# Linear attention, 32 heads: single warm-up matmuls, the first five heads reordered, and each store cut in three by partitions

## The chip, the core and the metric

The kernel runs on one core of one Trainium2 chip. The time is the device time of one execution in microseconds; the profile shows the core's five engines (PE, the matrix engine; DVE, ACT and POOL, which work on elements; SP, which here only issues DMA transfers) and the 16 DMA engines that move data between HBM and the on-chip memory.

## The reference

```python
# q, k, v: (1, 32, 2048, 128), bf16
phi_q = where(q > 0, q + 1, exp(q)) + 1e-6
phi_k = where(k > 0, k + 1, exp(k)) + 1e-6
kv  = einsum("bhsd,bhse->bhde", phi_k, v)
z   = einsum("bhsd->bhd", phi_k)
num = einsum("bhqd,bhde->bhqe", phi_q, kv)
den = einsum("bhqd,bhd->bhq", phi_q, z)[..., None] + 1e-6
return num / den
```

Each of the 32 heads is on its own: a sum over 2048 rows gives a 128 x 128 matrix kv and a vector z, and every row of q is then multiplied by them and divided.

## The kernel before

A head's q, k and v are 512 KB each and its output is 512 KB. All are laid out on 128 partitions with 16 rows of 128 values (4 KB) on each. The kernel is written out by hand: every piece of work has a name such as `kv3.0` (operation, head, part) and a list of the pieces that it waits for. `ORDER` holds one list per engine, in which that engine does its pieces strictly one after the other. Semaphore waits are made from these lists. So the order within an engine is fixed, and engines wait for one another only where data or a buffer requires it.

The pieces of a head h, with their lines in the profile:

- `ldk`, `ldq`, `ldv` (lines 343 to 348): load of k, q, v, 512 KB each, issued by SP (the v of head 0 by ACT). There are `NI` = 7 input buffers, so a load of head h waits until head h-7 has been used.
- `ek` (360, ACT): exp of k. `em` (363, DVE): min(exp, 1) + 1e-6, in place. `rkp` (370, POOL), and for half of head 0 `rkd` (366, DVE): max(k, 0). phi_k is em + rk, and the two are never added: both go through PE.
- `v1` (374, POOL): v copied beside a column of ones (`v1ones`, 324), so that z is column 128 of the product.
- `kv` (381, PE): 32 matmuls, 16 row blocks times two parts of phi_k, into one PSUM bank. `kvs` (386, DVE): that result to bf16 in the on-chip memory. `kv` of the next head waits for it.
- `T` (393, PE): 16 transposes of q into PSUM. `eq` (397, ACT), `emq` (399, DVE), `rqa` (403, ACT, first half) and `rqb` (406, DVE, second half): the two parts of phi_q from it. `T` of the next head waits for `eq`, `rqa` and `rqb`.
- `n` (417, 422, 424, PE): phi_q times (kv, z), in two groups (`n0.0` of 12 blocks, `n0.1` of 4). `a` (437), `r` (440), `f` (444), all DVE: epsilon, reciprocal, division out of PSUM into one of `NO` = 12 output buffers. `a` of the second group of head h also waits for `kv` of head h+2, because they share a PSUM bank.
- `st` (452, SP): store of the head's output, one transfer of 128 partitions (three for the last head).

Head 0 has k, v and the transposes in two halves. `warm` pieces `w` (329, PE) are matmuls on the identity that nobody uses; they keep PE busy before there is data. `WARM = (2, 8, 4)` is the number in each, and `w2 w1` stand ahead of the first transposes, `w0` behind them.

The program that stands around the orders adds the semaphores: each buffer's transfers count on a semaphore of their own (`o0` to `o11` for the outputs), and a store's completion frees its buffer 12 heads later.

Of the kernel before, what the change touches and what calls it, by code (L numbers as in the profile page):

```python
# [6 lines left out]
P = 128  # L7
EPS = 1e-6
ENGINES = ("PE", "DVE", "ACT", "POOL", "SP")
NH = 32  # L10
BY_ACT = ('ldv0.0',)
NI, NO, NE, NR, NV, NQ, NK = 7, 12, 2, 2, 2, 2, 2
WARM = (2, 8, 4)
HALVES = ((0, 8), (8, 16))
WHOLE = ((0, 16),)

# [41 lines left out]
def groups(h):  # L58
    if h == NH - 1:
        return ((0, 2, 3, 0), (6, 2, 3, 2), (12, 2, 2, 4))  # L60
    return ((0, 4, 3, 0), (12, 2, 2, 4))


def st_parts(h):
    return ((0, 6), (6, 12), (12, 16)) if h == NH - 1 else WHOLE


# [20 lines left out]
def rqb_parts(h):  # L88
    if na(h) == 16:
        return ()  # L90
    if h == NH - 1:
# [3 lines left out]

ORDER = {
    "PE": """
        w2 w1 T0.0 T0.1 w0 T1.0 kv0.0 kv0.1 n0.0 kv1.0 T2.0 n0.1 kv2.0 n1.0 n1.1 T3.0 kv3.0 n2.0 T4.0 n2.1 kv4.0
        n3.0 T5.0 n3.1 kv5.0 n4.0 T6.0 n4.1 kv6.0 n5.0 T7.0 n5.1 kv7.0 n6.0 T8.0 n6.1 kv8.0 n7.0 T9.0 n7.1 kv9.0
        n8.0 T10.0 n8.1 kv10.0 n9.0 T11.0 n9.1 kv11.0 n10.0 T12.0 n10.1 kv12.0 n11.0 T13.0 n11.1 kv13.0 n12.0  # L100
        T14.0 n12.1 kv14.0 n13.0 T15.0 n13.1 kv15.0 n14.0 T16.0 n14.1 kv16.0 n15.0 T17.0 n15.1 kv17.0 n16.0
        T18.0 n16.1 kv18.0 n17.0 T19.0 n17.1 kv19.0 n18.0 T20.0 n18.1 kv20.0 n19.0 T21.0 n19.1 kv21.0 n20.0
        T22.0 n20.1 kv22.0 n21.0 T23.0 n21.1 kv23.0 n22.0 T24.0 n22.1 kv24.0 n23.0 T25.0 n23.1 kv25.0 n24.0
        T26.0 n24.1 kv26.0 n25.0 T27.0 n25.1 kv27.0 n26.0 T28.0 n26.1 kv28.0 n27.0 T29.0 n27.1 kv29.0 n28.0
        T30.0 n28.1 kv30.0 n29.0 T31.0 T31.1 n29.1 kv31.0 n30.0 n30.1 n31.0 n31.1 n31.2
    """,
    "DVE": """
        eps0 ones emq0.0 em0.0 em0.1 rqb0.0 rkd0.0 v1ones0 v1ones1 eps1 emq0.1 em1.0 eps2 kvs0 emq1.0 r0.0
        rqb1.0 em2.0 kvs1 f0.0 em3.0 a0.1 r0.1 kvs2 f0.1 rqb2.0 r1.0 f1.0 emq2.0 em4.0 a1.1 r1.1 rqb3.0 f1.1
        r2.0 kvs3 f2.0 emq3.0 em5.0 a2.1 r2.1 rqb4.0 f2.1 r3.0 kvs4 f3.0 emq4.0 em6.0 a3.1 r3.1 rqb5.0 f3.1 r4.0  # L110
        kvs5 f4.0 emq5.0 em7.0 a4.1 r4.1 rqb6.0 f4.1 r5.0 kvs6 f5.0 emq6.0 em8.0 a5.1 r5.1 rqb7.0 f5.1 r6.0 kvs7
        f6.0 emq7.0 em9.0 a6.1 r6.1 rqb8.0 f6.1 r7.0 kvs8 f7.0 emq8.0 em10.0 a7.1 r7.1 rqb9.0 f7.1 r8.0 kvs9
        f8.0 emq9.0 em11.0 a8.1 r8.1 rqb10.0 f8.1 r9.0 kvs10 f9.0 emq10.0 em12.0 a9.1 r9.1 rqb11.0 f9.1 r10.0
        kvs11 f10.0 emq11.0 em13.0 a10.1 r10.1 rqb12.0 f10.1 r11.0 kvs12 f11.0 emq12.0 em14.0 a11.1 r11.1
        rqb13.0 f11.1 r12.0 kvs13 f12.0 emq13.0 em15.0 a12.1 r12.1 rqb14.0 f12.1 r13.0 kvs14 f13.0 emq14.0
        em16.0 a13.1 r13.1 rqb15.0 f13.1 r14.0 kvs15 f14.0 emq15.0 em17.0 a14.1 r14.1 rqb16.0 f14.1 r15.0 kvs16
        f15.0 emq16.0 em18.0 a15.1 r15.1 rqb17.0 f15.1 r16.0 kvs17 f16.0 emq17.0 em19.0 a16.1 r16.1 rqb18.0
        f16.1 r17.0 kvs18 f17.0 emq18.0 em20.0 a17.1 r17.1 rqb19.0 f17.1 r18.0 kvs19 f18.0 emq19.0 em21.0 a18.1
        r18.1 rqb20.0 f18.1 r19.0 kvs20 f19.0 emq20.0 em22.0 a19.1 r19.1 rqb21.0 f19.1 r20.0 kvs21 f20.0 emq21.0
        em23.0 a20.1 r20.1 rqb22.0 f20.1 r21.0 kvs22 f21.0 emq22.0 em24.0 a21.1 rqb23.0 r21.1 f21.1 r22.0 kvs23  # L120
        f22.0 emq23.0 em25.0 a22.1 r22.1 rqb24.0 f22.1 r23.0 kvs24 f23.0 emq24.0 em26.0 a23.1 r23.1 rqb25.0
        f23.1 r24.0 kvs25 f24.0 emq25.0 em27.0 a24.1 r24.1 rqb26.0 f24.1 r25.0 kvs26 f25.0 emq26.0 em28.0 a25.1
        r25.1 rqb27.0 f25.1 r26.0 kvs27 f26.0 emq27.0 em29.0 a26.1 r26.1 rqb28.0 f26.1 r27.0 kvs28 f27.0 emq28.0
        em30.0 a27.1 r27.1 rqb29.0 f27.1 kvs29 r28.0 emq29.0 f28.0 em31.0 a28.1 kvs30 rqb30.0 r28.1 f28.1 r29.0
        emq30.0 f29.0 emq31.0 emq31.1 a29.1 r29.1 kvs31 f29.1 emq31.2 r30.0 f30.0 a30.1 r30.1 f30.1 r31.0 f31.0
        a31.1 r31.1 r31.2 f31.1 f31.2
    """,
    "ACT": """
        exp ldv0.0 ek0.0 ek0.1 eq0.0 eq0.1 rqa0 ek1.0 eq1.0 ek2.0 rqa1 ek3.0 eq2.0 rqa2 ek4.0 eq3.0 rqa3 ek5.0
        eq4.0 rqa4 ek6.0 eq5.0 rqa5 ek7.0 eq6.0 rqa6 ek8.0 eq7.0 rqa7 ek9.0 eq8.0 rqa8 ek10.0 eq9.0 rqa9 ek11.0  # L130
        eq10.0 rqa10 ek12.0 eq11.0 rqa11 ek13.0 eq12.0 rqa12 ek14.0 eq13.0 rqa13 ek15.0 eq14.0 rqa14 ek16.0
        eq15.0 rqa15 ek17.0 eq16.0 rqa16 ek18.0 eq17.0 rqa17 ek19.0 eq18.0 rqa18 ek20.0 eq19.0 rqa19 ek21.0
# [2 lines left out]
        eq30.0 rqa30 eq31.0 eq31.1 eq31.2 rqa31  # L135
    """,
    "POOL": """
        ident0 ident rkp0.0 rkp1.0 v10.0 v10.1 v11.0 rkp2.0 v12.0 rkp3.0 v13.0 v14.0 rkp4.0 v15.0 rkp5.0 v16.0
        rkp6.0 v17.0 rkp7.0 rkp8.0 v18.0 rkp9.0 v19.0 rkp10.0 v110.0 v111.0 rkp11.0 v112.0 rkp12.0 v113.0
        rkp13.0 v114.0 rkp14.0 v115.0 rkp15.0 v116.0 rkp16.0 rkp17.0 v117.0 rkp18.0 v118.0 v119.0 rkp19.0 v120.0  # L140
        rkp20.0 rkp21.0 v121.0 rkp22.0 v122.0 rkp23.0 v123.0 rkp24.0 v124.0 rkp25.0 v125.0 v126.0 rkp26.0 v127.0
        rkp27.0 v128.0 rkp28.0 v129.0 rkp29.0 v130.0 rkp30.0 rkp31.0 v131.0
    """,
    "SP": """
        ldk0.0 ldq0.0 ldk1.0 ldk2.0 ldq1.0 ldv1.0 ldk3.0 ldv2.0 ldq2.0 ldq3.0 ldk4.0 ldv3.0 ldv4.0 ldv5.0 ldk5.0
        ldv6.0 ldq4.0 ldk6.0 ldq5.0 ldk7.0 ldv7.0 ldk8.0 ldk9.0 ldv8.0 ldq6.0 ldq7.0 ldk10.0 ldv9.0 st0.0 ldq8.0
        ldv10.0 ldv11.0 ldk11.0 ldq9.0 ldq10.0 ldv12.0 ldq11.0 ldk12.0 ldk13.0 ldv13.0 ldq12.0 ldq13.0 ldq14.0
        ldq15.0 ldv14.0 ldv15.0 ldq16.0 ldk14.0 ldk15.0 ldk16.0 ldv16.0 ldv17.0 ldk17.0 st1.0 st2.0 ldq17.0
        ldq18.0 ldk18.0 ldv18.0 ldk19.0 ldv19.0 ldk20.0 ldq19.0 st3.0 ldv20.0 ldv21.0 st4.0 ldq20.0 ldk21.0
        ldq21.0 st5.0 ldk22.0 st6.0 ldq22.0 st7.0 st8.0 ldv22.0 ldk23.0 ldk24.0 ldv23.0 ldk25.0 ldv24.0 ldk26.0  # L150
        ldv25.0 st9.0 ldq23.0 st10.0 st11.0 st12.0 ldq24.0 ldk27.0 ldv26.0 ldk28.0 ldq25.0 ldv27.0 st13.0
        ldk29.0 ldq26.0 ldq27.0 ldk30.0 ldv28.0 st14.0 ldv29.0 st15.0 ldq28.0 ldv30.0 ldq29.0 ldk31.0 st16.0
        ldq30.0 st17.0 st18.0 st19.0 ldv31.0 st20.0 ldq31.0 st21.0 st22.0 st23.0 st24.0 st25.0 st26.0 st27.0
        st28.0 st29.0 st30.0 st31.0 st31.1 st31.2
    """,
}

# [10 lines left out]
class Program:  # L168
# [10 lines left out]
    def add(self, eng, key, fn, deps=(), dma=None, inc=True):  # L179
        assert key not in self.op, key  # L180
        self.op[key] = (eng, fn, tuple(deps), dma, inc)
# [71 lines left out]
def bass_standalone__linear_attn_elu__prompt_kernel(nc: bass.Bass, q: bass.AP, k: bass.AP, v: bass.AP, out: bass.AP):  # L253
# [8 lines left out]
    qf, kf, vf, of = (t.rearrange("b h s d -> (b h) s d") for t in (q, k, v, out))  # L262
    rows = lambda t, h: t[h].rearrange("(p j) d -> p j d", j=NT)

    with ExitStack() as es:
# [17 lines left out]
        o_sb = sb([P, NO, NT, D])  # L283
        ident, ones, epsr = sb([P, P]), sb([P, P]), sb([P, 3])
# [7 lines left out]
        add = pr.add  # L292
# [33 lines left out]
        def warm(key, n):  # L326
            def g(e):
                for w in range(n):
                    ins = e.matmul(o_ps[:, 512:992], lhsT=ident[:], rhs=_ap(ident[:, :], 0, [[0, 4], [1, 120]]),  # L329
                                   start=(w == 0), stop=(w == n - 1))  # L330
                return ins
            add("PE", key, g, ["ident"], inc=False)

        for i, n in enumerate(WARM):
            warm(f"w{i}", n)
# [15 lines left out]
        def head(h):  # L351
# [58 lines left out]
            for i, (t0, nb, m, b0) in enumerate(groups(h)):  # L410
# [31 lines left out]
                def g(e, t0=t0, t1=t1, nb=nb, m=m, b0=b0):  # L442
# [5 lines left out]
                        in1=_ap(rden_sb[:, :, :], first(rden_sb[:, h % 2, t0:t0 + 1]) - first(rden_sb[:, :, :]),  # L448
                                [[m, nb], [1, m], [0, D]]), op=ALU.mult)
                add("DVE", f"f{h}.{i}", g, [f"r{h}.{i}"] + freed(NO, h, ("st", st_parts)))  # L450
            for i, (a, b) in enumerate(st_parts(h)):
                add("SP", f"st{h}.{i}", lambda e, a=a, b=b: e.dma_start(rows(of, h)[:, a:b], o_sb[:, h % NO, a:b]),
                    [f"f{h}.{j}" for j, (t0, nb, m, b0) in enumerate(groups(h)) if t0 < b and a < t0 + nb * m],
                    dma=f"o{h % NO}")

        for h in range(NH):
            head(h)
# [40 lines left out]
```

## Time and profile before

| | |
|---|---|
| median of 3 runs | 169.61 us (169.48 to 169.76) |
| the profiled execution | 170.02 us |
| its span, first to last instruction | 168.6 us |
| mean granted PE clock | 0.983 |
| busy: PE, DVE, ACT, POOL | 155.6, 153.7, 149.6, 93.4 us |
| moved by DMA | 67.51 MB, mean 400 GB/s |
| HBM read, written | 50.33 MB, 16.78 MB |

The span is the time between the first and the last instruction of the profiled execution. Busy time is the union of an engine's instructions. Matmuls are pipelined, so one that is listed with 220 ns starts about 56 ns after the one before it, and PE's pace is read from starts and not from durations. "GB/s" and the DMA share count what all 16 DMA engines move in a stretch; a share slightly over 1 means that packets overlap a little.

### The profile page before, as it was taken

The page shows a single profiled execution, that of the slowest core. Times are in us where ns is not written, and L with a number is a line of the kernel's source. Part 1 is how long each engine was busy: PE and PEld are TensorE (multiplying, and loading weights), DVE is VectorE, ACT ScalarE, POOL GpSimd, SP SyncE. Part 2 cuts the span into 40 slices and gives each one's busy share as a digit, 9 for nine tenths or more (in the row PEclk, how much of TensorE's full clock was granted, in tenths as well). Part 3 has the DMA queues.
Part 4 walks back from the last instruction along what each step waited for, and adds up shares of the span by engine and source line. Part 5 has one row for each costly group of instructions (what it writes and reads, how often), then busy time and mean ns, then how long its engine had stood idle before and what let it go on. Part 6 is the DMA issues. An engine that isn't in the chain of part 4 may idle for free.

```text
span 168.6 us, 6160 instructions
## 1 busy us (share of the span) xinstructions
PE 155.6 (92%) x2702; PEld 151.2 (90%) x2702; DVE 153.7 (91%) x300; ACT 149.6 (89%) x102; POOL 93.4 (55%) x71
## 2 busy tenths in 40 slices
PE   6809999999999999999999999999999999999940
PEld 2309999999999999999999999999999999999940
DVE  0093999999999999999999999999999999999993
ACT  3784799999999999999999999999999999996800
POOL 1380895566666555555566666555555667642000
PEclk9996999999999999999999999999999999999997
DMA  5999999999999999999999999999999999999985
GB/s 206 431 420 424 385 431 393 412 412 406 416 400 412 408 404 408 390 436 402 395 429 419 408 421 425 417 389 430 433 406 404 412 445 390 420 417 414 391 326 225
DMA packets 9819, 67.51 MB, mean 400 GB/s; under 512 B 2080, under 2 KB 2464, under 8 KB 6816
## 3 DMA queue, kind: packets, MB, share of 16 engines
q1 hardware_dynamic: 9648, 66.59, 96.8%
q8 instruction: 21, 0.34, 0.8%
q10 hardware_dynamic: 144, 0.52, 0.8%
q14 instruction: 6, 0.05, 0.1%
HBM read 50.33 MB, written 16.78 MB: 398 GB/s over the span
## 4 chain that ended last, share of the span: by engine, by line
PE 88%; DVE 6%; DMA 3%; ACT 1%; issue 0%; SPq 0%
PE la L381 35%; PE la L422 18%; PE la L393 17%; PE la L424 17%; DMA la<-in_q_dram 3%; DVE la L444 3%; DVE la L399 1%; DVE la L363 1%; ACT la L397 1%; DVE la L440 1%; PE la L417 0%; DVE la L406 0%; SPq L348 0%; DVE la L386 0%; DVE la L437 0%
## 5 line engine op out<-in xcount | busy, mean ns | idle before, releaser
L444 DVE TENSOR_TENSOR la<-la 128x1536 bf16<-128x1536 f32 (+2 forms) x65 | 77.7, 1197 | 0.2
L370 POOL TENSOR_SCALAR la<-la 128x2048 bf16<-128x2048 bf16 (+1 forms) x32 | 59.7, 1866 | 29.3 <-PE la L381 23.8
L424 PE MATMUL la<-la 128*128 128x129 bf16 x512 | 67.0, 220 | 0.0
L422 PE MATMUL la<-la 128*128 128x129 bf16 x512 | 67.0, 219 | 0.0
L397 ACT ACTIVATE la<-la 128x2048 bf16<-128x2048 bf16 (+2 forms) x35 | 60.2, 1730 | 6.0 <-PE la L393 3.3
L360 ACT ACTIVATE la<-la 128x2048 bf16<-128x2048 bf16 (+1 forms) x33 | 61.3, 1860 | 3.8 <-PE la L381 2.0
L381 PE MATMUL la<-la 128*128 128x129 bf16 x1024 | 64.4, 222 | 0.0
L381 PEld LDWEIGHTS la<-la 128*128 128x128 bf16 x1024 | 60.5, 99 | 0.0
L374 POOL COPY la<-la 128x1024 int32<-128x1024 int32 (+1 forms) x33 | 34.4, 1043 | 29.5 <-PE la L381 25.5
L424 PEld LDWEIGHTS la<-la 128*128 128x128 bf16 x512 | 49.6, 97 | 0.0
L422 PEld LDWEIGHTS la<-la 128*128 128x128 bf16 x512 | 47.9, 97 | 0.2 <-DVE la L444 0.2
L393 PE MATMUL la<-la 128*128 128x128 bf16 x512 | 34.5, 222 | 4.6 <-DVE la L406 4.2
L393 PEld LDWEIGHTS la<-la 128*128 128x128 bf16 x512 | 30.4, 99 | 5.8 <-ACT la L360 4.6
L403 ACT ACTIVATE la<-la 128x1024 bf16<-128x1024 bf16 (+1 forms) x32 | 33.5, 1046 | 0.0
L399 DVE TENSOR_SCALAR la<-la 128x2048 bf16<-128x2048 bf16 (+2 forms) x35 | 25.3, 724 | 7.3 <-ACT la L397 7.3
L363 DVE TENSOR_SCALAR la<-la 128x2048 bf16<-128x2048 bf16 (+1 forms) x33 | 23.9, 726 | 0.0
L417 PE MATMUL la<-la 128*128 128x3 bf16 (+1 forms) x128 | 21.6, 169 | 2.1 <-DVE la L444 1.7
L406 DVE TENSOR_SCALAR la<-la 128x1024 bf16<-128x1024 bf16 x31 | 20.5, 662 | 0.0
L417 PEld LDWEIGHTS la<-la 128*128 128x128 bf16 x128 | 12.5, 98 | 2.4 <-DVE la L444 1.8
L440 DVE RECIPROCAL la<-la 128x12 f32<-128x12 f32 (+2 forms) x65 | 13.0, 201 | 1.1
L386 DVE CAST la<-la 128x129 bf16<-128x129 f32 x32 | 7.8, 243 | 2.6 <-PE la L381 2.6
L329 PE MATMUL la<-la 128*128 128x480 bf16 x14 | 5.2, 546 | 1.5 <-POOL la L314 1.5
(16 smaller groups left out, 10.7 us busy)
## 6 DMA issues: line engine op xcount, KB each, us to landing
la<-in_k_dram SPq DMA_DIRECT2D x32, 512.0 KB, 17.5
la<-in_q_dram SPq DMA_DIRECT2D x32, 512.0 KB, 18.2
la<-in_v_dram SPq DMA_DIRECT2D x31, 512.0 KB, 18.5
out_dram<-la SPq DMA_DIRECT2D x31, 512.0 KB, 19.1
la<-in_v_dram ACTq DMA_DIRECT2D x1, 512.0 KB, 4.9
out_dram<-la SPq DMA_DIRECT2D x2, 192.0 KB, 2.6
out_dram<-la SPq DMA_DIRECT2D x1, 128.0 KB, 2.8
```

The lines of the kernel that those rows point to most:

```text
L360: add("ACT", f"ek{h}.{i}", lambda e, a=a, b=b: e.activation(em_sb[:, h % NE, a:b], k_sb[:, h % NI, a:b], ACT.Exp), over("ldk", h, ld_parts ...
L370: add("POOL", f"rkp{h}.{i}", lambda e, a=a, b=b: e.tensor_scalar(rk_sb[:, h % NR, a:b], k_sb[:, h % NI, a:b], BIG, 0.0, op0=ALU.min, op1=A ...
L374: add("POOL", f"v1{h}.{i}", lambda e, a=a, b=b: e.tensor_copy(v1_sb[:, h % NV, a:b, 0:D].bitcast(i32), v_sb[:, h % NI, a:b].bitcast(i32)), ...
L381: ins = e.matmul(kv_ps, lhsT=src[:, j], rhs=v1_sb[:, h % NV, j, 0:NC], start=(j + part == 0), stop=(j == NT - 1 and part == 1))
L393: ins = e.transpose(xT[:, j], q_sb[:, h % NI, j], ident[:])
L397: add("ACT", f"eq{h}.{i}", lambda e, a=a, b=b: e.activation(emq_sb[:, h % NQ, a:b], xT[:, a:b], ACT.Exp), over("T", h, t_parts, a, b) + fr ...
L399: add("DVE", f"emq{h}.{i}", lambda e, a=a, b=b: e.tensor_scalar(emq_sb[:, h % NQ, a:b], emq_sb[:, h % NQ, a:b], 1.0, EPS, op0=ALU.min, op1 ...
L403: add("ACT", f"rqa{h}", lambda e: e.activation(rq_sb[:, h % NQ, 0:n], xT[:, 0:n], ACT.Relu), over("T", h, t_parts, 0, n) + freed(NQ, h, (" ...
L417: e.matmul(_ap(o_ps[:, :], o + D, [[NC, m]]), lhsT=ones[:], rhs=epsr[:, 0:m], start=True, stop=False, skip_group_check=True)
L422: e.matmul(to, lhsT=emq_sb[:, h % NQ, t], rhs=kvs_sb[:, h % NK, 0:NC], start=late and c == 0, stop=False, skip_group_check=True)
L424: ins = e.matmul(to, lhsT=rq_sb[:, h % NQ, t], rhs=kvs_sb[:, h % NK, 0:NC], start=False, stop=True, skip_group_check=True)
L444: return e.tensor_tensor(out=_ap(o_sb[:, :, :, :], first(o_sb[:, h % NO, t0, 0:1]) - first(o_sb[:, :, :, :]), [[m * D, nb], [D, m], [1, D] ...
```

## The change

Three things are changed.

The warm-up becomes 17 pieces: sixteen of a single matmul and one of 12. The piece of 12 and nine single ones stand ahead of the first transposes, two behind each half of these and four between `kv0.1` and `T1.0` (28 matmuls in all instead of 14).

The orders of the first five heads are new on all engines. On PE, `kv0` stands ahead of `T1.0`; on ACT, `ek1.0` ahead of `eq0.0`; on DVE, the memsets, `em0.0`, `rkd0.0` and `em0.1` ahead of `emq0.0`. On POOL, `rkp` and `v1` alternate through nearly all heads.

The stores of heads 0 to 21 become three transfers each, of partitions 0 to 47, 48 to 95 and 96 to 127, whole rows of 4 KB as before. In SP's order they stand between the loads from the 16th SP transfer on. Before, `st0.0` came behind 28 loads and `st1.0` behind 24 more.

```diff
-WARM = (2, 8, 4)
+WARM = (1, 1, 1, 1, 1, 1, 1, 1, 1, 1, 1, 1, 1, 1, 1, 1, 12)
...
+ROWS = ((0, 48), (48, 96), (96, 128))
+
+def st_rows(h, i):
+    return ROWS[i] if len(st_parts(h)) == len(ROWS) and h < NH - 1 else (0, P)
+
 def st_parts(h):
+    if h < 22:
+        return WHOLE * len(ROWS)
     return ((0, 6), (6, 12), (12, 16)) if h == NH - 1 else WHOLE
...
 PE
-        w2 w1 T0.0 T0.1 w0 T1.0 kv0.0 kv0.1 n0.0 kv1.0 T2.0 n0.1 kv2.0 n1.0 n1.1 T3.0 kv3.0 n2.0 T4.0 n2.1 kv4.0
+        w16 w6 w4 w7 w8 w9 w1 w10 w11 w12 T0.0 w0 w13 T0.1 w2 kv0.0 kv0.1 w14 w5 w3 w15 T1.0 kv1.0 n0.0 n0.1
+        T2.0 kv2.0 n1.0 T3.0 n1.1 kv3.0 n2.0 T4.0 n2.1 kv4.0 ...
 DVE
-        eps0 ones emq0.0 em0.0 em0.1 rqb0.0 rkd0.0 v1ones0 v1ones1 eps1 emq0.1 em1.0 eps2 kvs0 emq1.0 r0.0
-        rqb1.0 em2.0 kvs1 f0.0 em3.0 a0.1 r0.1 kvs2 f0.1 rqb2.0 r1.0 f1.0 ...
+        v1ones0 eps0 v1ones1 eps1 ones em0.0 rkd0.0 eps2 em0.1 emq0.0 em1.0 rqb0.0 emq0.1 kvs0 em2.0 kvs1 rqb1.0
+        r0.0 f0.0 emq1.0 em3.0 a0.1 r0.1 rqb2.0 f0.1 r1.0 kvs2 f1.0 ...
 ACT
-        exp ldv0.0 ek0.0 ek0.1 eq0.0 eq0.1 rqa0 ek1.0 eq1.0 ek2.0 rqa1 ek3.0 ...
+        exp ldv0.0 ek0.0 ek0.1 ek1.0 eq0.0 eq0.1 rqa0 ek2.0 eq1.0 rqa1 ek3.0 ...
 SP
-        ldk0.0 ldq0.0 ldk1.0 ldk2.0 ldq1.0 ldv1.0 ldk3.0 ldv2.0 ldq2.0 ldq3.0 ldk4.0 ldv3.0 ldv4.0 ldv5.0 ldk5.0
-        ldv6.0 ldq4.0 ldk6.0 ldq5.0 ldk7.0 ldv7.0 ldk8.0 ldk9.0 ldv8.0 ldq6.0 ldq7.0 ldk10.0 ldv9.0 st0.0 ldq8.0
...
-        ldq30.0 st17.0 st18.0 st19.0 ldv31.0 st20.0 ldq31.0 st21.0 st22.0 st23.0 ...
+        ldk0.0 ldq0.0 ldk1.0 ldk2.0 ldv1.0 ldq1.0 ldv2.0 ldk3.0 ldq2.0 ldv3.0 ldq3.0 ldk4.0 ldv4.0 ldk5.0 ldq4.0
+        st0.0 ldv5.0 ldq5.0 st0.1 ldk6.0 ldq6.0 st0.2 ldv6.0 st1.0 ldk7.0 ldv7.0 st1.1 ldq7.0 ldk8.0 st1.2
...
+        st17.1 st17.2 ldq29.0 st18.0 st18.1 st18.2 ldk31.0 st19.0 ldq30.0 st19.1 st19.2 st20.0 ldq31.0 st20.1
+        st20.2 st21.0 ldv31.0 st21.1 st21.2 st22.0 st23.0 ...
...
-                add("SP", f"st{h}.{i}", lambda e, a=a, b=b: e.dma_start(rows(of, h)[:, a:b], o_sb[:, h % NO, a:b]),
+                add("SP", f"st{h}.{i}", lambda e, a=a, b=b, p=st_rows(h, i): e.dma_start(
+                    rows(of, h)[p[0]:p[1], a:b], o_sb[p[0]:p[1], h % NO, a:b]),
                     [f"f{h}.{j}" for j, (t0, nb, m, b0) in enumerate(groups(h)) if t0 < b and a < t0 + nb * m],
```

## The prediction

> **What bounds the kernel now.** I read the page first (queues, slices), then the windows view by stage, then the chain and the timelines of the start. The page's DMA queues and its slices of DMA share and rate:
>
> ```profile
> q1 hardware_dynamic: 9648, 66.59, 96.8%
> q8 instruction: 21, 0.34, 0.8%
> ...
> DMA  5999999999999999999999999999999999999985
> GB/s 206 431 420 424 385 431 393 412 412 406 416 400 412 408 404 408 390 436 402 395 429 419 408 421 425 417 389 430 433 406 404 412 445 390 420 417 414 391 326 225
> ```
>
> The 16 DMA engines idle only in the first slice and the last two. By stage (stretch, length, busy time of PE, PEld, DVE, ACT, POOL; granted clock, DMA share, GB/s):
>
> ```profile
> 12.00:16.00 4.00, 3.69 (x37) 3.72 (x38) 2.17 (x8) 1.88 (x1) 0.80 (x1) 0.57 0.98 397
> 43.00:57.00 14.00, 14.00 (x258) 14.00 (x256) 13.90 (x29) 13.90 (x10) 8.78 (x7) 1.00 1.01 407
> 73.00:100.00 27.00, 27.00 (x495) 27.00 (x493) 26.80 (x55) 26.82 (x19) 16.61 (x13) 1.00 1.02 416
> 100.00:122.00 22.00, 22.00 (x404) 22.00 (x402) 21.86 (x43) 21.84 (x15) 13.28 (x10) 1.00 1.02 420
> 160.00:166.00 6.00, 2.19 (x38) 1.91 (x36) 5.65 (x11) 0.19 (x1) 0.00 (x0) 1.00 0.80 320
> ```
>
> PE, DVE, ACT and DMA are all full. A stretch of loads alone (43 to 57) moves 407 GB/s, loads mixed with stores 416 to 420. At 414 GB/s the 67.1 MB need 162 us from the first packet at 1.8, so 4 to 5 us of the span is all that DMA has to spare, most of it at the end.
>
> PE's own clock is set at the start. The chain in order of time (start, length, what) has T1.0 at 12.31 and then the kv matmuls of heads 0, 1, 3 and 4:
>
> ```profile
> 12.31 1.66 PE la L393 x16
> 13.97 2.85 PE la L381 x32
> 18.83 1.81 PE la L381 x32
> 26.93 1.81 PE la L381 x32
> 31.55 1.81 PE la L381 x32
> ```
>
> T1.0 and kv0 run at half clock (0.57 above) after 4.2 us of idle PE; from head 3 on a head takes 4.62 us with no gap until 160. DVE's timeline shows what the start waits for: emq0.0, which takes 1.77 us where its twin emq0.1 takes 0.41, because it ends only after POOL's rkp1.0 has (9.84).
>
> ```profile
> 8.35 1.77 DVE L399 TENSOR_SCALAR la<-la 128x1024 bf16<-128x1024 bf16 x1 [7.32 <-ACT la L397]
> 16.84 0.30 DVE L386 CAST la<-la 128x129 bf16<-128x129 f32 x1 [2.62 <-PE la L381]
> ```
>
> Which of the two clocks sets the end? Each transfer's semaphore is raised 16 times, once by each DMA engine, and the trace records each. The slowest engine finishes ldq31.0 (the 117th transfer) at 154.35 and the last store at 168.59: 13 transfers of 11 stores' bytes, 1.29 us per store, no gap. DMA sets the end, and PE's last work arrives just in time for it.
>
> **Warm-up and first heads.** T0.0 now stands behind 12 warm-up matmuls (end near 6.0, as before) and 9 more at 0.20 us (line 329 at full clock): 7.8 instead of 6.63. That is hidden: ACT does ek1.0 first, from k1's landing (7.9) to 9.75, so eq0.0 begins there. If the clock came late, 9 at 0.40 would add 1.8 us, and eq0.0 would move by 0.1. kv0 no longer waits for T1.0: its last input is v10.0, half of a 1.04 us copy behind rkp1.0, so it begins near 10.5 and ends at 12.3, not 16.8. T1.0 waits for rqb0.0 behind em1.0: 13.5. kv1 waits for kvs0, which DVE has behind emq0.1, which waits for POOL's rkp2.0 to end (14.7): kv1 at 15.3. From there, with 1.81 for kv, 0.89 for T and 4.62-1.81-0.89 = 1.92 for n, kv3 begins 9.24 us later, at 24.5 instead of 26.93. PE gains 2.4 us, some 1.8 of it the cold clock ((1.66-0.89) + (2.85-1.81)). The POOL reorder costs nothing (55% busy), nor do the memsets put first on DVE, idle until 5. It is worth 2.4 us only if loads and stores keep up.
>
> The Trainium skill, "TensorE: Matmul & The Clock Gate", part 1, has the clock fall after an idle window of about 3.4 us, so the gaps of about 1 us left here would be harmless; no row here has such a gap that early.
>
> **st0 on SP's queue.** SP issues in order. Before, st0 was the 29th transfer on SP, waiting until 25.24 with some 18 us of loads already queued. Now 16 loads are issued by 10 and SP stops at st0.0, with ldv5.0 and all later loads behind it. st0.0 waits for f0.1, whose a0.1 waits for kv2 (ends 15.3+1.81+1.92+0.89+1.81 = 21.7); a, r, rqb2.0 and f0.1 make it 23.45. The 16th load lands at 23.1 on the median engine. A store of 192 KB into an empty queue first lands 1.8 us after issue (the last head's, 163.93 to 165.76), so at 25.3; without a gap it would have landed at 23.1+0.48. Idle DMA: 1.7, say 1.8 us; 1.1 on an engine that lags (its 16th load lands at 24.4). Bounds: 0.8 if f0.1 comes a microsecond earlier, 2.8 if later. Nothing hides it, as DMA sets the end. From there st1.0 finds 3 us queued: no second gap.
>
> **Splitting and interleaving.** From one transfer's landing on the fastest engine to the next one's, 6th to 119th transfer:
>
> ```
> previous, this    times  us after the previous one
> load, load           75  1.272
> load, store          16  1.249
> store, load          15  1.199
> store, store          7  1.231
> ```
>
> A load behind a store is 0.073 us cheaper, a store behind a load 0.018 dearer than behind a store. In the stages with many stores a load takes 1.25 to 1.26 even behind a load; I take 1.25. From st0's place to the end of st21 the old order has 80 loads and 22 stores, 22.84 to 150.86 = 128.0 us. In the new one 56 loads stand directly behind a store part, 24 behind a load; 57 parts behind a load. So 56 x 1.199 + 24 x 1.25 + 22 x 1.231 + 57 x 0.018 = 67.1 + 30.0 + 27.1 + 1.0 = 125.2: 2.8 us less. 44 more semaphore packets at 9 ns each per engine: +0.4. No row shows a store of 48 or 32 partitions, nor a load behind one. Bounds for such a load: 1.199 if the saving belongs to the change of direction, 1.248 if it goes by bytes (a third of 0.073). I take the first: after three stores in a row (st10 to st12, then ldq24.0) it is 1.21, no better than after one. SP's 44 further issues of 0.35 us fit into its waits.
>
> Sum: -2.8 + 0.4 + 1.8 = -0.6 us. The last load is ldv31.0, behind 21 3/8 stores where ldq31.0 had 21: it lands at 154.35 - 0.6 + 0.5 = 154.2, v131 takes 1.04, so kv31 begins at 155.4, 0.8 earlier than now: PE agrees with DMA. The other 1.6 us that PE could gain go into waiting for loads, at lines 360, 370, 374 or 393.
>
> The Trainium skill, "DMA: Bandwidth & Descriptors", rules for kernel authors, speaks against the split: two transfers to disjoint partitions share the same 16 engines, so use one of 128 partitions. By that rule alone the split brings nothing and the sum is that of the first rival; the rows above favour it only as mixing.
>
> The profiled execution took 170.02 us, 1.4 more than its span of 168.6, and lies 0.41 above the median of 169.61; the change is taken against that median: 169.0.
>
> **Rivals.** *Slower: the cheaper load goes by bytes.* 56 x 0.049 = +2.7, so +2.1: 171.7. It decides once a load behind a part takes over 1.210 us (1.199 + 0.6/56). For it: the trace's 16 KB load packets take 637 ns with no store packet beside them and 614 to 628 with some, so it is company that helps, and a third of a store gives it a third as long. Chance 0.30. *Slower: parts of 48 partitions move more slowly than 159 ns per 4 KB packet*, the figure of every store here. Each 10% costs 22 x 1.27 x 0.1 = 2.8 us; it decides from 2%. Nothing in the profile shows it. 172 and more, chance 0.10. *Much faster: DMA stops being the bound*, with 1.20 for every load (-1.2 more) and half of the gap. Then PE's 2.4 us hold: 167.2. Chance 0.12. *No change:* the terms cancel within 0.34 us, the 0.2% that a measurement of this kernel can tell: 0.14.
>
> **Numbers.** Forecast 169.0, chance 0.34 (168.0 to 169.2). Range 167.2 to 171.8: it leaves out the slow parts and little else. Faster 0.34 + 0.12, same 0.14, slower 0.30 + 0.10.
>
> **What would show it.** Right: clock 1.00 from 12 to 16; kv1 near 15.3, kv3 near 24.5; st0.0 issued near 23.5 and a dip of the DMA share around 23 to 25; 418 GB/s or more from 26 to 150; heads a little over 4.62 us apart with waits for loads. Wrong: 410 GB/s or less in that stretch (first rival), store packets over 159 ns (second), 4.62 us per head to the end (third), or no dip.

## The result, and the profile after

The changed kernel takes 172.55 us (172.52 to 172.92, 4 runs) against 169.67 us (169.48 to 169.76, 4 runs) for the kernel before on the same chip: ratio 1.0169, 95% interval 1.0154 to 1.0184. It is 2.9 us slower; the forecast was 169.0, and the time lies above the range. The profiled execution took 172.52 us, its span is 171.2 us (168.6 before), and the mean granted clock is 0.997 (0.983 before). In the views of the changed kernel the lines are 12 or 13 further down: `ek` is 373, `rkp` 383, `v1` 387, `kv` 394, `T` 406, `eq` 410, `emq` 412.

The start first. The chain in order of time of the changed kernel (start, length, what), from ACT's `ek1.0` to `kv1`:

```profile
8.25 1.45 ACT la L373
9.70 0.37 issue
10.07 1.01 ACT la L410
11.10 0.47 DVE la L412
11.58 1.44 DVE la L376
13.02 0.60 DVE la L419
13.62 1.51 DVE la L412
15.12 0.21 DVE la L399
15.38 1.99 PE la L394 x32
```

It is the chain that the prediction described: `emq0.1` (13.62) takes 1.51 us where `emq0.0` takes 0.47, while POOL is in `rkp2.0` (12.95 to 14.84); `kvs0` (15.12) stands behind it, and `kv1` starts at 15.38.

The changed kernel's DMA queues and slices show what went wrong:

```profile
q1 hardware_dynamic: 10352, 66.60, 95.7%
q8 instruction: 21, 0.34, 0.8%
...
DMA  5999959999999999999999999999999999999976
GB/s 208 424 417 413 410 178 313 368 438 398 441 414 412 412 420 419 416 418 412 419 418 415 428 395 433 404 419 427 411 420 428 409 409 421 421 407 406 400 310 240
```

A slice is 4.28 us. The DMA share has one hole, in the sixth slice (178 GB/s), but the next two slices, with the engines busy again by their share, still move only 313 and 368. The windows view of the changed kernel (stretch, length, busy time of PE, PEld, DVE, ACT, POOL; granted clock, DMA share, GB/s):

```profile
12.00:16.00 4.00, 3.36 (x47) 2.51 (x45) 4.00 (x5) 4.00 (x3) 3.52 (x3) 1.00 0.99 401
20.00:24.00 4.00, 4.00 (x77) 4.00 (x75) 3.97 (x10) 3.78 (x3) 2.25 (x3) 1.00 0.63 254
24.00:28.00 4.00, 4.00 (x77) 4.00 (x75) 3.97 (x7) 3.97 (x4) 2.25 (x2) 1.00 0.91 262
28.00:32.00 4.00, 4.00 (x77) 4.00 (x75) 3.96 (x9) 3.97 (x3) 1.58 (x2) 1.00 0.98 344
32.00:36.00 4.00, 4.00 (x76) 4.00 (x73) 4.00 (x8) 3.92 (x4) 1.97 (x2) 1.00 1.00 414
43.00:57.00 14.00, 12.84 (x227) 12.31 (x225) 13.93 (x24) 12.39 (x9) 9.05 (x7) 1.00 1.01 416
73.00:100.00 27.00, 27.00 (x494) 27.00 (x492) 26.79 (x53) 26.81 (x18) 16.52 (x13) 1.00 1.01 416
100.00:122.00 22.00, 22.00 (x403) 22.00 (x401) 21.86 (x43) 20.78 (x15) 12.99 (x9) 1.00 1.02 418
160.00:166.00 6.00, 4.28 (x74) 3.76 (x72) 5.83 (x15) 2.65 (x3) 0.00 (x0) 1.00 0.85 343
```

From 12 to 16 PE now has the full clock (0.57 before). From 28 to 32 the DMA share is 0.98 at 344 GB/s: busy engines, slow packets. From 43 to 122 the rate is 416 to 418, and in 43 to 57 PE is idle 1.2 of 14 us where it had no idle before.

PE's inputs come late: POOL and ACT, which prepare them, wait longer for loads. The waits view covers the whole span (us in total, times, longest). Of the changed kernel:

```profile
POOL la L383 <- DMA la<-in_k_dram: 22.8, 11, 3.8
POOL la L387 <- DMA la<-in_v_dram: 7.8, 4, 4.1
ACT la L373 <- DMA la<-in_k_dram: 6.7, 5, 2.1
```

and of the kernel before:

```profile
POOL la L370 <- DMA la<-in_k_dram: 5.4, 2, 2.8
POOL la L374 <- DMA la<-in_v_dram: 3.9, 3, 2.5
ACT la L360 <- DMA la<-in_k_dram: 1.9, 1, 1.9
```

PE's 2.2 us lead over the kernel before is there until head 6 (`kv6` at 38.50 against 40.71), is gone at head 9, and is a delay of 1.40 us from head 10 and of 2.45 us at the last (`kv31` at 158.67 against 156.22).

What DMA has moved for loads and stores, from the packet records of both traces:

```
MB moved by            34 us   60 us   100 us   150 us
before                 13.02   23.57    39.96    60.65
after                  11.46   22.28    38.85    59.58
behind, MB              1.56    1.29     1.11     1.07
the same at 414 GB/s   3.8 us  3.1 us   2.7 us   2.6 us
```

All of the loss is there at 34 us; after that the new order gains 1.2 us back. 2.6 us are left, and 2.6 us is what the span has grown by.

### The profile page after: what moved, and what is told of

Same layout as the page of the kernel before. It is cut to its first block, busy times and chain, and to the rows that moved or that the text cites. A ratio compares the mean times of both kernels' runs of the same rounds, so it can differ in the third digit from the quotient of the medians.

```text
span 171.2 us, 6223 instructions
## 1 busy us (share of the span) xinstructions
PE 158.3 (92%) x2716; PEld 151.1 (88%) x2716; DVE 155.7 (91%) x300; ACT 149.7 (87%) x102; POOL 95.1 (56%) x71
## 4 chain that ended last, share of the span: by engine, by line
DVE 65%; PE 24%; DMA 4%; ACT 4%; issue 2%; SPq 0%
DVE la L457 30%; DVE la L376 10%; PE la L394 10%; DVE la L412 10%; DVE la L419 8%; PE la L406 5%; PE la L435 5%; PE la L437 4%; DVE la L453 4%; DMA la<-in_k_dram 4%; DVE la L399 2%; ACT la L410 2%; DVE la L450 1%; ACT la L416 1%; ACT la L373 1%
## 5 line engine op out<-in xcount | busy, mean ns | idle before, releaser
L383 POOL TENSOR_SCALAR la<-la 128x2048 bf16<-128x2048 bf16 (+1 forms) x32 | 60.8, 1901 | 53.2 <-PE la L394 30.4
L394 PEld LDWEIGHTS la<-la 128*128 128x128 bf16 x1024 | 59.2, 98 | 2.2 <-issue 1.3
L437 PEld LDWEIGHTS la<-la 128*128 128x128 bf16 x512 | 49.5, 97 | 0.0
L435 PEld LDWEIGHTS la<-la 128*128 128x128 bf16 x512 | 47.8, 97 | 0.3 <-DVE la L399 0.3
L387 POOL COPY la<-la 128x1024 int32<-128x1024 int32 (+1 forms) x33 | 35.0, 1064 | 9.5 <-DMA la<-in_v_dram 7.8
L406 PE MATMUL la<-la 128*128 128x128 bf16 x512 | 34.0, 219 | 2.9 <-DVE la L419 1.9
L406 PEld LDWEIGHTS la<-la 128*128 128x128 bf16 x512 | 29.8, 98 | 4.5 <-DVE la L419 2.9
L376 DVE TENSOR_SCALAR la<-la 128x2048 bf16<-128x2048 bf16 (+1 forms) x33 | 26.1, 791 | 4.1 <-ACT la L373 4.0
L430 PEld LDWEIGHTS la<-la 128*128 128x128 bf16 x128 | 12.5, 97 | 3.0 <-DVE la L457 2.0
L342 PE MATMUL la<-la 128*128 128x480 bf16 x28 | 8.7, 469 | 1.5 <-POOL la L327 1.5
```

What stands on the lines that cost most here:

```text
L376: add("DVE", f"em{h}.{i}", lambda e, a=a, b=b: e.tensor_scalar(em_sb[:, h % NE, a:b], em_sb[:, h % NE, a:b], 1.0, EPS, op0=ALU.min, op1=AL ...
L383: add("POOL", f"rkp{h}.{i}", lambda e, a=a, b=b: e.tensor_scalar(rk_sb[:, h % NR, a:b], k_sb[:, h % NI, a:b], BIG, 0.0, op0=ALU.min, op1=A ...
L387: add("POOL", f"v1{h}.{i}", lambda e, a=a, b=b: e.tensor_copy(v1_sb[:, h % NV, a:b, 0:D].bitcast(i32), v_sb[:, h % NI, a:b].bitcast(i32)), ...
L394: ins = e.matmul(kv_ps, lhsT=src[:, j], rhs=v1_sb[:, h % NV, j, 0:NC], start=(j + part == 0), stop=(j == NT - 1 and part == 1))
L406: ins = e.transpose(xT[:, j], q_sb[:, h % NI, j], ident[:])
L435: e.matmul(to, lhsT=emq_sb[:, h % NQ, t], rhs=kvs_sb[:, h % NK, 0:NC], start=late and c == 0, stop=False, skip_group_check=True)
```

## The experiments

Three theories: the gap behind `st0.0` and the slow stretch that follows it cost the time (A); the parts of 48 and 32 partitions do (B); the new start does (C). Within A: is it the stop itself, or something that comes with it? Each kernel is compared with the kernel before, run beside it on the same chip (median 169.95 us for runs 1 to 4, 170.05 for 5 to 8, 170.03 for 9 to 11, 169.89 for 12).

**1. The start alone.** The changed kernel with SP's order of before and whole stores.

```diff
 def st_parts(h):
-    if h < 22:
-        return WHOLE * len(ROWS)
...
 SP
-        ldk0.0 ldq0.0 ldk1.0 ldk2.0 ldv1.0 ldq1.0 ... ldk5.0 ldq4.0 st0.0 ldv5.0 ldq5.0 st0.1 ...
+        ldk0.0 ldq0.0 ldk1.0 ldk2.0 ldq1.0 ldv1.0 ... ldk10.0 ldv9.0 st0.0 ldq8.0 ldv10.0 ldv11.0 ...
...
```

> The new warm-up and the new orders of PE, DVE, ACT and POOL, with the old order of SP and whole stores. Theory A (the loss sits in the DMA gap behind st0.0, 22 to 34 us, and in what it costs to start again): st0 has its 23 loads ahead, no gap, kv3 near 24.6 as in the changed kernel, and PE keeps its lead of about 2 us as long as the loads of the old order allow: 167.5 to 169.3 us. Theory B (the split transfers are slow in themselves): the same here, since nothing is split. Theory C (the new start costs more than it saves, for instance by making every later wait fall badly): 170 us or more.

Measured 169.78 us, ratio 0.9993 (0.9983 to 1.0004). `kv3` is 3.2 us earlier than before, `kv10` still 1.85, and from head 24 on the lead melts: `kv31` is 0.28 later. The windows view of this kernel has PE waiting in 122 to 148:

```profile
122.00:148.00 26.00, 24.74 (x444) 24.30 (x442) 24.20 (x47) 23.87 (x17) 14.75 (x11) 1.00 1.01 414
```

The time lies between what A and C forecast. The start costs nothing (not C) and, with DMA's order unchanged, brings nothing: PE runs into DMA. The transposes of heads 24, 25, 26 and 28 each start 0.09 us after their q has landed (`T28` at 141.11, its q at 141.02). In the kernel before, `T28` starts at 141.01 with its q there since 140.75, so the old order of loads has hardly any lead to give.

**2. Whole stores at the new places.** The changed kernel, each store of heads 0 to 21 whole at its first part's place.

```diff
-    if h < 22:
-        return WHOLE * len(ROWS)
...
-        ... st0.0 ldv5.0 ldq5.0 st0.1 ldk6.0 ldq6.0 st0.2 ldv6.0 st1.0 ...
+        ... st0.0 ldv5.0 ldq5.0 ldk6.0 ldq6.0 ldv6.0 st1.0 ...
```

> The changed kernel with each store of heads 0 to 21 whole, in the place of its first part; the loads stay in their order. Theory A: the gap behind st0.0 stays, with about 4 us of DMA work lost in it, and there are fewer changes of direction: 172 to 174 us, DMA at 250 to 350 GB/s from 24 to 32 us. Theory B: the parts were the cost, so 170 us or less, and the rate after the gap comes back at once.

Measured 173.28 us, ratio 1.0198 (1.0166 to 1.0229). The windows view of this kernel shows the same hole and the same slow stretch without any part:

```profile
20.00:24.00 4.00, 4.00 (x77) 4.00 (x75) 3.96 (x10) 3.76 (x3) 2.25 (x3) 1.00 0.62 250
24.00:28.00 4.00, 4.00 (x77) 4.00 (x75) 3.97 (x7) 3.97 (x4) 2.26 (x3) 1.00 0.93 336
28.00:32.00 4.00, 4.00 (x76) 4.00 (x74) 3.96 (x9) 3.97 (x3) 2.12 (x3) 1.00 0.94 336
32.00:36.00 4.00, 4.00 (x75) 4.00 (x74) 4.00 (x8) 3.97 (x4) 1.38 (x1) 1.00 0.97 358
```

The parts are not the cause of the hole or of the slow stretch (not B).

**3. Stores eight loads later.** The changed kernel, parts and all, with `st0.0` behind 24 loads instead of 16; the shift shrinks evenly to none at `st21`.

```diff
-        ... ldk5.0 ldq4.0 st0.0 ldv5.0 ldq5.0 st0.1 ldk6.0 ldq6.0 st0.2 ldv6.0 st1.0 ...
+        ... ldk5.0 ldq4.0 ldv5.0 ldq5.0 ldk6.0 ldq6.0 ldv6.0 ldk7.0 ldv7.0 ldq7.0 st0.0 ldk8.0 ldq8.0 st0.1 ...
```

> The changed kernel, parts and all, but the stores stand eight loads later in SP's order at st0 (23 loads ahead of it, as in the old order), falling to none at st21. Theory A: no gap, DMA over 400 GB/s from 20 to 34 us, 172.55 minus about 4, held by PE's lead of 2.2 us over the kernel before: 167.4 to 169.0 us. Theory B: the parts are still there, so 171.5 us or more.

Measured 169.14 us, ratio 0.9970 (0.9950 to 0.9990). SP issues `st0.0` at 23.60, as in the changed kernel, but has transfers queued to 33. The windows view of this kernel:

```profile
20.00:24.00 4.00, 4.00 (x77) 4.00 (x74) 3.96 (x10) 3.79 (x3) 2.25 (x3) 1.00 1.00 406
24.00:28.00 4.00, 4.00 (x77) 4.00 (x74) 3.97 (x7) 3.97 (x4) 2.25 (x2) 1.00 1.00 401
28.00:32.00 4.00, 4.00 (x77) 4.00 (x75) 3.97 (x9) 3.97 (x3) 2.25 (x3) 1.00 1.00 406
```

Without the gap the change is faster than the kernel before. A holds.

**4. The split in place.** The kernel before, each store of heads 0 to 21 as three parts in a row where the whole one stood.

```diff
+    if h < 22:
+        return WHOLE * len(ROWS)
...
-        ... ldv9.0 st0.0 ldq8.0 ldv10.0 ...
+        ... ldv9.0 st0.0 st0.1 st0.2 ldq8.0 ldv10.0 ...
```

> The kernel before in all its orders, with the stores of heads 0 to 21 each in three parts, one behind the other in the place of the whole store. Only the split is new. Theory A: 44 more semaphore packets of 9 ns on each engine, 169.6 to 170.3 us. Theory B: packets of over 159 ns or more loss between parts, 171.5 us or more.

Measured 171.11 us, ratio 1.0068 (1.0047 to 1.0089). By itself this doesn't decide: `kv1` is already 1.2 us late (19.89 against 18.67), before any store is issued, with a granted clock of 0.68 in 16 to 20 where the kernel before has 1.00. The clock can't be all of it: with the same mean clock of 0.982 this kernel took 170.82 us and the kernel before, on the same chip, 169.85 and 169.91. Run 8 repeats the split without the cold stretch.

**5. The gap alone.** The kernel before, with the whole `st0.0` moved ahead.

```diff
-        ... ldv5.0 ldk5.0 ldv6.0 ldq4.0 ldk6.0 ldq5.0 ... ldv9.0 st0.0 ldq8.0 ...
+        ... ldv5.0 ldk5.0 st0.0 ldv6.0 ldq4.0 ldk6.0 ldq5.0 ... ldv9.0 ldq8.0 ...
```

> The kernel before with one edit: the whole store st0.0 is put behind 16 loads instead of 29, everything else as before. If the time goes into the stop behind st0.0 (no load can be issued until f0.1) and a slow restart of the DMA engines after it, the rate falls below 300 GB/s for some 4 us around 25 and stays under 380 to about 34, some 4 us of loads are missing, and the time is 172.5 to 174 (f0.1 ends 1.8 us later here than in the changed kernel, so the stop is longer). If the slow stretch belongs to the parts and their alternation with loads, the restart is at full rate at once, only the idle 2 to 3 us is lost, and the time is 171 to 172. If a stop at this point is hidden, 169.9.

Measured 175.84 us, ratio 1.0329 (1.0288 to 1.0371): moving one store costs 5.8 us. The windows view of this kernel:

```profile
20.00:24.00 4.00, 4.00 (x75) 4.00 (x73) 4.00 (x7) 2.98 (x3) 3.49 (x3) 1.00 0.65 258
24.00:28.00 4.00, 4.00 (x71) 3.68 (x69) 3.93 (x8) 4.00 (x4) 3.36 (x3) 1.00 0.32 119
28.00:32.00 4.00, 2.99 (x55) 2.81 (x52) 3.96 (x10) 4.00 (x3) 2.40 (x2) 1.00 1.07 287
32.00:36.00 4.00, 2.61 (x32) 2.64 (x33) 2.33 (x3) 0.87 (x2) 0.49 (x1) 0.77 0.99 418
```

The loss was expected at some 2.5 to 4 us and is larger: `st0.0` is issued at 26.02 here, 2.4 later than in the changed kernel, and the DMA engines idle twice as long (4.1 us against 2.05, see run 9). The slow stretch is there with one whole store and only loads behind it (28 to 32: share 1.07, 287 GB/s); the loss at 34 us is 2.37 MB, 5.7 us.

**6 and 7. Whole stores, eight later; parts, fourteen later.** Run 3 with whole stores:

```diff
-        ... ldq7.0 st0.0 ldk8.0 ldq8.0 st0.1 ldv8.0 ldk9.0 st0.2 ldq9.0 st1.0 ...
+        ... ldq7.0 st0.0 ldk8.0 ldq8.0 ldv8.0 ldk9.0 ldq9.0 st1.0 ...
```

and run 3 with a shift of 14 instead of 8:

```diff
-        ... ldq7.0 st0.0 ldk8.0 ldq8.0 st0.1 ldv8.0 ...
+        ... ldq7.0 ldk8.0 ldq8.0 ldv8.0 ldk9.0 ldq9.0 ldv9.0 st0.0 ldv10.0 ldk10.0 st0.1 ...
```

> The version with the stores eight loads later (169.14), but with each store of heads 0 to 21 whole at its first part's place. If splitting is what mixes loads and stores well, this is slower: by the prediction's terms 57 and more part landings lose up to 2 us, so 170 to 171. If the split is worth the 0.7 us that whole stores cost in the changed kernel, 169.8. If it is only the order of the stores that counts, 169.1, and the parts' 44 extra semaphore packets (0.4 us) show as 168.8.

> The version with the stores of 48, 48 and 32 partitions, first store behind 30 loads (14 later than in the changed kernel) in place of 24. If 24 loads already cover the wait for f0.1 completely, further delay brings nothing: 169.1. If the loads are still short of time in the heads 3 to 10, it gains up to 0.5: 168.6. If stores put off crowd the end, where no load is left to mix with, it loses up to 0.5: 169.6.

Measured 169.52 us, ratio 0.9962 (0.9949 to 0.9974), and 169.32 us, ratio 0.9952 (0.9940 to 0.9964). Whole or in parts makes no difference that the times resolve, and neither does a shift of 8 or 14. What gains over run 1 (0.9993) is where the stores stand, not that they are cut.

**8. The new start and the split in place.** Run 1 with three parts in a row.

```diff
+    if h < 22:
+        return WHOLE * len(ROWS)
...
-        ... ldv9.0 st0.0 ldq8.0 ldv10.0 ...
+        ... ldv9.0 st0.0 st0.1 st0.2 ldq8.0 ldv10.0 ...
```

> The changed kernel's warm-up and first heads with the SP order of the kernel before, each store of heads 0 to 21 as three parts in a row. It is the start-only version (169.78) plus the split alone, without the cold clock at 12 to 20 that disturbed the earlier split-in-place version (171.11). If parts cost their 44 extra semaphore packets, 170.2; if parts are slow by themselves, 171 and more; if a split store costs nothing, 169.8; if the start of the other version made its whole 1.2 us, this stays within 0.3 of 169.8.

Measured 170.89 us, ratio 1.0058 (1.0035 to 1.0081), where run 1 had 0.9993: parts in a row cost some 1.1 us. The 4 KB packets take 159 ns as ever. `st22.0` lands 0.29 us later than in run 1 on the fastest engine and 0.37 on the median one, near the 0.4 reckoned for 44 more semaphore packets; on the slowest engine it is 1.08. Why the slowest engine loses more stays open.

**9 and 10. Two and four loads later.** How much must be queued when SP stops? With 18 loads ahead of `st0.0` they last just to the moment (25.5) at which the store's own bytes begin to move; with 20, some 2.5 us longer.

```diff
-        ... ldq4.0 st0.0 ldv5.0 ldq5.0 st0.1 ldk6.0 ...
+        ... ldq4.0 ldv5.0 ldq5.0 st0.0 ldk6.0 ldq6.0 st0.1 ...
```

```diff
-        ... ldq4.0 st0.0 ldv5.0 ldq5.0 st0.1 ldk6.0 ...
+        ... ldq4.0 ldv5.0 ldq5.0 ldk6.0 ldq6.0 st0.0 ldv6.0 ldk7.0 st0.1 ...
```

> The changed kernel with its stores two loads later: st0.0 stands behind 18 loads, which last to about 25.4, the moment at which the first bytes of a store issued at 23.6 can land, so hardly any idle is left (0.5 us or less), but next to nothing is queued when the loads behind it are issued. If only the empty queue costs time, or packets are slow because the DMA engines had stopped, the loss goes with the idle: under 0.7 us, so 169.2 to 169.9. If packets are slow whenever only one or two transfers are queued, the 16 KB packets of 25 to 33 still take 0.7 us and more, some 1.5 us are lost, and the time is 170.4 to 171.

> The same with four loads: st0.0 behind 20 loads, which last to about 28, so 3 us of transfers are queued when it is issued. If only idle counts, 169.1 to 169.4, like eight loads. If a short queue counts, something between: 0.3 to 0.8 us lost, 169.5 to 169.9.

Measured 169.98 us, ratio 0.9995 (0.9984 to 1.0006), and 169.01 us, ratio 0.9941 (0.9927 to 0.9955). The windows view with two loads:

```profile
24.00:28.00 4.00, 4.00 (x77) 4.00 (x75) 3.97 (x7) 3.97 (x4) 2.25 (x2) 1.00 1.03 361
28.00:32.00 4.00, 4.00 (x77) 4.00 (x74) 3.97 (x9) 3.97 (x3) 2.25 (x3) 1.00 0.94 364
```

and with four:

```profile
24.00:28.00 4.00, 4.00 (x76) 4.00 (x74) 3.97 (x7) 3.97 (x4) 2.25 (x2) 1.00 1.00 402
28.00:32.00 4.00, 4.00 (x76) 4.00 (x74) 3.97 (x9) 3.97 (x3) 2.25 (x3) 1.00 1.03 427
```

The time of run 9 lies between its two expected ranges, so the packets have to decide. With two loads more the engines hardly stop and the rate is still only 361 to 364. From the packet records, between 22 and 36 us (idle is per DMA engine; "over" is the time of the 16 KB packets beyond 625 ns, per engine):

```
                      idle us   16 KB packets   over 700 ns   longest ns   over, us   MB by 34 us
before                   0.00             345             2         1118       0.35         13.02
changed                  2.05             213            60         1579       1.34         11.46
gap alone (5)            4.11             178            29         2339       1.44         10.65
two later (9)            0.04             287            38         1891       0.97         12.60
four later (10)          0.00             308             2         1114       0.20         13.03
```

Run 9 separates the two costs: next to no idle (0.04 us), and still 38 slow packets and 0.42 MB, 1.0 us, behind. That is also the difference of the two runs, 0.97 us. So the second cost belongs to the short queue and not to the stop. The 0.3 to 0.8 us that run 10 was expected to lose if a short queue counts did not come: its queue was already long enough. On the fastest DMA engine of the changed kernel the loads `ldv5.0` to `ldq6.0` land 3.3, 4.1, 5.1 and 6.1 us after their issue, and all of their stretch is slow; in run 9 the slow ones (`ldk6.0`, `ldq6.0`, `ldv6.0`, `ldk7.0`) land after 3.5 to 4.9 us; in run 10 `ldv6.0` lands after 5.7 and is at full speed.

**11. Whole stores, fourteen later.** Run 7 with whole stores.

```diff
-        ... ldv9.0 st0.0 ldv10.0 ldk10.0 st0.1 ldk11.0 ldk12.0 st0.2 st1.0 ...
+        ... ldv9.0 st0.0 ldv10.0 ldk10.0 ldk11.0 ldk12.0 st1.0 ...
```

> The 14-loads-later version (ratio 0.9952) with whole stores, the candidate for the best. If splitting is worth nothing once there is no gap, as eight loads later suggests (0.9962 whole, 0.9970 in parts), this is 0.994 to 0.996, 169.2. If parts bring 0.2% or more there, 169.6.

Measured 169.36 us, ratio 0.9961 (0.9949 to 0.9974): as with parts (0.9952).

**12. The old start with the stores eight later.** Run 3 with the warm-up and the PE, DVE, ACT and POOL orders of before.

```diff
-WARM = (1, 1, 1, 1, 1, 1, 1, 1, 1, 1, 1, 1, 1, 1, 1, 1, 12)
+WARM = (2, 8, 4)
...
 PE
-        w16 w6 w4 w7 w8 w9 w1 w10 w11 w12 T0.0 w0 w13 T0.1 w2 kv0.0 kv0.1 w14 w5 w3 w15 T1.0 kv1.0 n0.0 n0.1 ...
+        w2 w1 T0.0 T0.1 w0 T1.0 kv0.0 kv0.1 n0.0 kv1.0 T2.0 n0.1 kv2.0 n1.0 n1.1 T3.0 kv3.0 n2.0 ...
...
```

> The eight-loads-later version (ratio 0.9970) with the warm-up and the first heads of the kernel before: the PE, DVE, ACT and POOL orders and the warm-up line are the old ones, the stores and SP's order are not. f0.1 ends at 25.2 in the old start against 23.57, but 23 loads last to 33, so no gap opens. If DMA alone sets the end, the start is worth nothing here either: 0.996 to 0.998, about 169.4. If PE's 2 us head start is what lets the transfers keep up at the end, it loses 0.5 to 2 us: 1.000 to 1.008, about 170 to 171. A cold clock at 12 to 20 as in the first split-in-place version would add up to 1.2 us of PE time.

Measured 169.88 us, ratio 0.9999 (0.9985 to 1.0013). The windows view of this kernel:

```profile
122.00:148.00 26.00, 26.00 (x477) 26.00 (x474) 25.79 (x51) 25.82 (x18) 17.27 (x12) 1.00 1.02 418
148.00:158.00 10.00, 10.00 (x185) 10.00 (x183) 9.93 (x20) 8.14 (x7) 3.03 (x2) 1.00 1.01 402
158.00:164.00 6.00, 4.34 (x82) 4.16 (x80) 5.77 (x15) 2.70 (x3) 0.00 (x0) 1.00 0.72 288
```

and that of run 3 has, for the last stretch:

```profile
158.00:164.00 6.00, 3.79 (x64) 3.27 (x62) 5.83 (x16) 0.75 (x1) 0.00 (x0) 1.00 0.82 331
```

Now PE is never idle from 122 to 158 (in run 1 it was idle 1.3 us there), and DMA is, with a share of 0.72 in 158 to 164 where run 3 has 0.82: PE has become the bound. The clock fits this: of this kernel's 12 executions the three with a mean granted clock of 0.985 to 0.987 took 169.22 to 169.49 us, the nine with 0.975 to 0.979 took 169.60 to 170.27. The better start alone is worth nothing (run 1), the better store order alone is worth nothing (this run), and both together are worth 0.3 to 0.6% (runs 3 and 10). The intervals of run 12 and run 3, which differ in the start alone, still overlap a little (0.9985 to 1.0013 and 0.9950 to 0.9990).

## Why the prediction was wrong

**Right: the start.** `kv0` at 10.9 (near 10.5 forecast), `T1.0` 13.7 (13.5), `kv1` 15.4 (15.3), `kv3` 24.6 (24.5), the clock 1.00 from 12 to 16, `st0.0` issued at 23.61 (23.45). That the gain would be lost in waits for loads came true, at lines 373, 383 and 387 after. No gap of PE between its warm-up and `kv3` is over 1.1 us, and the clock stayed at 1.00; where the old start idles PE for 4.2 us, as in run 12, the clock fell to 0.50. The Trainium skill, "TensorE: Matmul & The Clock Gate", part 1, which has the clock fall after an idle window of about 3.4 us, agrees with both.

**Right: the idle.** 1.8 us were reckoned (0.8 to 2.8), and the trace has 2.05 us per engine.

**Wrong, and the step that turned the sign: "Idle DMA: 1.7, say 1.8 us" as the whole price of the stop, followed by "From there st1.0 finds 3 us queued: no second gap".** There is no second stop, but the sum went on at full rate from the store's landing, and the DMA engines did not. The loads issued right behind the store found next to nothing queued, and their packets took up to 1.58 us instead of 0.61 to 0.64: 1.34 us per engine. The first part's own packets (212 to 335 ns at the median of their half microseconds, instead of 159) add some 0.4. With the idle that makes 3.8 us, which is what the bytes show at 34, and twice the term. The bounds of 0.8 and 2.8 moved only the issue of the store and did not contain this. The last head's store, from which the landing time was taken, has nothing behind it, so its row could not show it.

**Wrong in size: mixing.** -2.8 + 0.4 = -2.4 us was reckoned; from 34 to 150 the new order gains 0.49 MB, 1.2 us. The sign named for it, 418 GB/s or more from 26 to 150, reads 413 there, with the slow stretch in it, and 418 from 34, where the kernel before has 413. The cadence of the fastest engine shows which number failed. Between 40 and 150 us of the changed kernel a load lands 1.250 us behind a load, as taken. With a 48-partition part between them two loads land 1.712 us apart, which leaves 1.23 for the load after the part's own 0.486 (three packets of 159 ns and a semaphore packet of 9), where 1.199 was taken; with a 32-partition part it is 1.552 and 0.327, so 1.23 again. That is the first rival's condition (over 1.210), but not its figure (1.248). At 0.026 us more, 56 such loads lose 1.5 of the 2.4 us. By this the order gains 0.9 us and by the bytes 1.2, about halfway between the forecast (-2.4) and the first rival (+0.3). The rate is 416 in 43 to 57, where there had been only loads at 407, and 416 to 418 from 73 to 122, where it had been 416 to 420 already: in these stretches mixing is worth something only where there had been none.

**The sum**: +3.8 - 1.2 = +2.6 where -0.6 stood. With the mixing as forecast the change would still have been 1.4 us slower, so the first step alone turns the sign.

**The rivals.** None named the cause, which runs 2, 3 and 5 show to be the gap and the restart behind it. The first (171.7) had the right condition, and of its 2.7 us some 1.2 to 1.5 came. The second has the time (172 and more) by luck: beyond the restart the parts' packets take 159 ns. The third needed DMA to stop being the bound. Run 12 shows that with the old start; with the new one, in run 10, POOL still waits 13.6 us for k at line 383. The Trainium skill, "DMA: Bandwidth & Descriptors", rules for kernel authors, says that transfers to disjoint partitions are better made as one. Runs 6 and 11 agree as far as they resolve (0.9962 and 0.9961 whole, 0.9970 and 0.9952 in parts), and run 8, with the parts in a row, shows a price of 0.65%.

The version of run 10, four loads later, beats both kernels: 169.01 us, ratio 0.9941.

## What to carry to other kernels

Where one queue issues both loads and stores, a store that waits for a result stops all loads behind it, so it belongs behind as many loads as cover the wait and the time until the loads behind it run at full rate: here 20 loads ahead (2.5 us more than just enough) were enough, 18 cost 1 us and 16 cost 3.8 us. A gap in a resource that is the bound costs its idle time and its restart; cost both, and look for the restart in a row that has something queued behind the gap. Where two clocks, PE and DMA, end together, improving one shows nothing: try the two improvements together before dropping either.

## What the runs showed of the hardware that was not expected

A DMA engine that is busy by its share may still move up to a third less (287 GB/s at a share of 1.07 in run 5). The 16 KB packets behind it took 0.7 to 2.3 us instead of 0.61 to 0.64: 60 of 213 in the changed kernel, 38 of 287 in run 9 with 0.04 us of idle, 2 of 308 in run 10. The slow loads had been issued shortly before their turn and landed 3.3 to 6.1 us after their issue. A load that landed after 5.7 us was at full speed in run 10, so the border lies near 5 us and is not sharp. What the packets wait for, no run tells.

At full rate a 16 KB load packet takes some 640 ns beside other loads and 613 to 625 beside stores (medians, kernel before). How the store bytes are cut makes little difference to it: 616 to 621 beside stores in run 3, with parts, and 621 to 625 in run 6, with whole stores.
